# Sequence 0's chosen rows transposed by VectorE from gathered quarter rows, and a regular order of step 4's values

## The chip, the cores and the metric

The kernel runs on one core of a Trainium2 chip. The metric is the device time of one launch in microseconds; before the change its median over 3 runs is 431.92 us (431.19 to 432.13). All data are float32.

## The reference, cut to what matters

```python
# attention: 8 sequences, 12 heads, 448 tokens, head size 64
scores = q @ k.T / sqrt(64) - log(448)
x = sigmoid(scores) @ v                  # heads joined: x is (8, 448, 768)
# mixture of depths, for each sequence b
s = x[b] @ w_gate                        # one score for each token
top_idx = argpartition(-s, 128)[:128]    # the 128 best tokens
xe = x[b, top_idx]                       # (128, 768): the "chosen rows"
ye = relu(xe @ w1) @ w2                  # w1 (768, 1024), w2 (1024, 768)
out[b, top_idx] = xe + sigmoid(s[top_idx])[:, None] * ye
out[b, others] = x[b, others]
```

## The kernel before, in words

**Steps and slots.** Attention is done in 12 steps (s = 0 to 11), each on two groups of four heads. A step has 7 slots (n = 0 to 6). A slot makes scores on TensorE into two PSUM tiles of two banks each, `PA[0]` and `PA[1]` (`score`, L387, matmuls on L397), ScalarE turns each tile by a sigmoid into `attn` (`squash`, L402, L411), and TensorE multiplies earlier `attn` tiles with v into four PSUM banks `PO[x][pr]` (`value`, L416, L429). The values run behind the scores: the values of step s run from slot 4 of step s to slot 3 of step s+1. A score call uses half of the 128 rows of TensorE's array and a value call the other half, so that a score and a value can run side by side; two scores of the same `pr` or two values of the same half go one after the other.

**Three orders of values.** `slot` (L856) has: (1) the regular order of `rounds` (L777), in which one slot near the end of a step's values is split (`split`, L785): there both halves of the values are started before the scores and ended after them; (2) for the steps in `LATE` (L788), `first_slots` and `last_slot` with the tables `LOW` and `HIGH`; (3) one for step 0. `LATE` is steps 4 to 10 before the change. For steps whose successor is in `BLOCKS` (L706) the split is the last slot, otherwise the last but one. When all values of a step are in, VectorE transposes them out of `PO` into `x_b` (`take`, L447, L453). TensorE cannot write a bank of `PO` for the next step until that is done. `join` (L435) writes one element of each `PO` bank on ScalarE or VectorE, which fixes the order between engines.

**Blocks of the second part.** In slot 3 of steps 4 to 11, `block` (L736) runs takes, stores, parts of the gate and the items of `BLOCKS[s]`: ("t", b) transposes the chosen rows of sequence b, (1, p, key) and (2, p, key) are quarter-size products of the first and second matrix for a pair p of sequences (seven products in place of eight, by sums of quarters). Each item takes PSUM banks from `places`. Step 4 held only ("t", 0), and step 5 held (1, 0, 1) and (1, 0, 2), 48 matmuls together.

**Chosen rows.** `fetch(b)` (L540) on VectorE makes the list of 128 token numbers `idx`; `gather(b)` reads these rows of 3072 bytes from `out` into `xe`, by an indirect DMA issued on GpSimd. `turn_rows` (L568) transposes `xe` by six TensorE transposes of 128 columns each (L580) into two PSUM banks, which ScalarE copies into the tile `rows_t` (L582, L583); a third ScalarE instruction makes the gate (L585). In the transpose, `xe` is the stationary operand and the identity the moving one. `rows_t` also serves as v of steps 1 and 3, so it is free only when the values of step 3 are done.

**Order.** The whole order is written out by hand (`tc.manual_schedule`): each engine works through its own list in the order of the calls. DMAs go out on SP's queue (loads of q, k, weights; stores), on GpSimd's (ranks, gathers) and a few on ScalarE's. `after` (L973) says what follows each slot.

Of the kernel before, what the change touches and what calls it, by code (L numbers as in the profile page):

```python
# [17 lines left out]
def kernel(  # L18
# [170 lines left out]
    def load_v(s, pairs_too=None):  # L189


        if s >= NS:
            return
        if s == 0 and not pairs_too:
            t = raw_v[s]
        elif s in (1, 3):
            t = moe.tile([P, 6 * KH * P], F32, name="rows_t")[:, :4 * NU * Dh]
        elif s == min(BLOCKS) + 1:
# [33 lines left out]
    sums = {}  # L232
    lent = {}

    def quarter(m, i, j):

        if m == 1:
            return moe_w1[j * KH * P:(j + 1) * KH * P, i * FH * P:(i + 1) * FH * P].rearrange(
                "(t p) c -> p t c", p=P)
        return moe_w2[i * FH * P:(i + 1) * FH * P, j * DH:(j + 1) * DH].rearrange(  # L240
            "(t p) c -> p t c", p=P)

    HELD1, HELD2 = ((0, 0), (0, 1), (1, 1)), ((0, 0), (1, 0), (1, 1))

    def load_quarter(m, dst, at):
        nc.sync.dma_start(out=dst.rearrange("p (t c) -> p t c", t=KH if m == 1 else FH),
                          in_=quarter(m, *at))

    def load_held(m, x):
        load_quarter(m, (w1_sb, w2_sb)[m - 1][:, x], (HELD1, HELD2)[m - 1][x])  # L250
# [77 lines left out]
    who = [const.tile([P, NC], F32, name=f"who{x}") for x in range(2)]  # L328
    tokens = const.tile([P, TB, TT], F32, name="tokens")
    slot_s = const.tile([P, 1], F32, name="slot_s")  # L330
    gate_s = const.tile([P, TT], F32, name="gate_s")
    place_s = const.tile([P, TT], F32, name="place_s")

    def constants():
        make_identity(nc, iden)
        nc.gpsimd.iota(slot_s, pattern=[[0, 1]], base=0, channel_multiplier=1,
                       allow_small_or_imprecise_dtypes=True)

        for t in (gate_s, *who):
            nc.gpsimd.memset(t, 0.0)  # L340
        nc.gpsimd.memset(place_s, float(S))
        nc.gpsimd.iota(tokens, pattern=[[1, TB], [TB, TT]], base=0, channel_multiplier=0,
                       allow_small_or_imprecise_dtypes=True)
# [196 lines left out]
    def fetch(b):  # L540
# [4 lines left out]
        for x, t in enumerate((tokens.rearrange("p r t -> p (r t)"), st[b]["rep"])):  # L545
# [4 lines left out]
        nc.vector.tensor_scalar(out=idx[:n], in0=got[:n, 0:1], scalar1=float(b * S),  # L550
                                scalar2=None, op0=ALU.add)
        st[b].update(idx=idx, picked=got[:, 1:2])
        gather(b)

    def gather(b):
# [9 lines left out]

    pairs = {}

    def turn_rows(b, both):  # L568


        n = CAP
# [4 lines left out]
        x = pairs[p]["x"]  # L576
        ps = [t.rearrange("p (k n) -> p k n", n=P) for t in both]
        for t in range(KD):
            a, i = divmod(t, KH)
            nc.tensor.transpose(ps[a][:, i, :n], st[b]["xe"][:n, t * P:(t + 1) * P],  # L580
                                iden[:n, :n])
        nc.scalar.activation(x[:, 2 * odd, :, :n], ps[0][:, :KH, :n], AF.Copy)  # L582
        nc.scalar.activation(x[:, 2 * odd + 1, :, :n], ps[1][:, :KH, :n], AF.Copy)  # L583
        st[b]["gate"] = moe.tile([P, 1], F32, name="gate", bufs=4)
        nc.scalar.activation(st[b]["gate"][:n], st[b]["picked"][:n], AF.Sigmoid,  # L585
                             scale=1.0 / GATE_UP)
        if not odd:
            return
        for dst, y, z in ((4, 2, 0), (5, 3, 4), (2, 3, 2)):
# [108 lines left out]
    def scatter(b):  # L698
# [5 lines left out]


    BLOCKS = {  # L706
# [29 lines left out]
    def block(s):  # L736

        places = [PO[0][0], PO[0][1], PA[1][:, 0], PA[0][:, 0], PO[1][0], PO[1][1], PO[1][0]]
        if s == NF + 1:
            places = [PA[1][:, 0], PO[0][0]]  # L740
        elif s == NF + 2:
            places = [PO[0][0], PO[1][0]]
        for x in range(2):
            takes(s - 1, x)
        if (s, NF) in FETCHED and s > NF + 3:
# [31 lines left out]
    def rounds(s):  # L777


        same = [(0, 0, 1), (1, 0, 1), (1, 2, 3), (0, 2, 3), (0, 4, 5)]  # L780
        if s + 1 in BLOCKS:
            return same + [(1, 4, 5), (1, 0, 6)]
        return same + [(0, 1, 6), (1, 4, 5)]

    def split(s, i):  # L785
        return i == (6 if s + 1 in BLOCKS else 5)

    LATE = range(min(BLOCKS), NS - 1)  # L788
# [67 lines left out]
    def slot(s, n):  # L856
# [22 lines left out]
        if vs in LATE and n == NF:  # L879
            last_slot(s, n)  # L880
            return
        if vs and vs not in LATE and split(vs, i):
            one, two, u = rounds(vs)[i]
            for half in range(2):
                value(vs, half, one, u)
# [87 lines left out]
    def after(s, n):  # L973

        if n == NF and s:
# [5 lines left out]
            if s in BLOCKS:  # L981
                block(s)
            else:
                stores(s, n)
            if s == 2:
                gates(2 * s - 2, own=False)
            else:
                turn("q", 2 * s + 2)
# [45 lines left out]
            keep_sum(m, key)  # L1034
        if (s, n) in MADE:
            make_sum(*MADE[s, n])
        for b in range(B - 1):
            full = FULL[b]
            if (s, n) == ((4, 0) if b == 1 else (full, 5 + b % 2)):
                spread(b)  # L1040
            if (s, n) == RANKED[b]:
                ranking(b)
# [67 lines left out]
```

## Time and profile before

| What | us |
|---|---|
| median of 3 runs | 431.92 (431.19 to 432.13) |
| the profiled execution | 434.43 |
| its span, first to last instruction | 432.6 |
| TensorE matmul busy in the span | 424.7 (98%) |
| VectorE busy | 281.6 (65%) |
| ScalarE busy | 190.3 (44%) |
| GpSimd busy | 48.0 (11%) |
| granted TensorE clock, mean | 1.000 |

The profiled execution is some 2.5 us longer than the median of the timed runs; 1.8 us of it lie outside its span. A step of the attention part shows as 14 sigmoids of ScalarE; the distance from one sigmoid to the same one of the next step is the length of a step, and reads any change of a step directly. TensorE runs several small matmuls at once, so its busy share says little: lost time shows as a longer distance between such marks, not as idle time.

### The profile page before, as it was taken

To read this page: it belongs to the slowest core of one execution; us is meant where nothing else is said; L and a number is where in the kernel's file an instruction comes from. 1 tells how busy PE (TensorE), PEld (TensorE's weight loads), DVE (VectorE), ACT (ScalarE), POOL (GpSimd) and SP (SyncE) were. 2 spreads that over 40 slices of the span, in tenths; PEclk is the share of its full clock that TensorE was granted. 3 is DMA by queue.
4 is the path that set the end of the run, shared out by engine and by line. 5 is a ranking of instruction groups with operands and counts; after the bars stand their busy time and mean duration, and the time that the engine had idled before them with its cause. 6 is when DMAs were issued, how large, how long until landed. Compare 5 with 4: busy or idle time off the path is not lost.

```text
span 432.6 us, 14250 instructions
## 1 busy us (share of the span) xinstructions
PE 424.7 (98%) x6324; PEld 254.7 (59%) x6324; DVE 281.6 (65%) x597; ACT 190.3 (44%) x249; POOL 48.0 (11%) x81
## 2 busy tenths in 40 slices
PE   8999999999999999999999999999999999999995
PEld 3455453545666478465447549546545859769952
DVE  4427557583967776976968636755666648983472
ACT  4666656666664633650660651563264330101100
POOL 3000001210210020100302020010020110101001
PEclk9999999999999999999999999999999999999999
DMA  6896747899863997988566887399935981821001
GB/s 191 245 273 178 285 89 155 207 209 251 252 180 74 244 296 186 261 269 204 182 224 184 240 204 152 103 265 277 264 109 116 236 241 36 162 57 77 23 1 73
DMA packets 114937, 78.64 MB, mean 182 GB/s; under 512 B 91420, under 2 KB 100892, under 8 KB 114876
## 3 DMA queue, kind: packets, MB, share of 16 engines
q1 hardware_dynamic: 107948, 62.47, 55.0%
q0 software_dynamic: 3296, 9.54, 7.6%
q10 hardware_dynamic: 3632, 5.74, 5.4%
q8 instruction: 49, 0.80, 0.8%
q14 instruction: 12, 0.10, 0.1%
HBM read 57.25 MB, written 20.48 MB: 180 GB/s over the span
## 4 chain that ended last, share of the span: by engine, by line
PE 93%; DMA 3%; ACT 1%; issue 1%; SPq 1%; DVE 1%; POOLq 0%; ACTq 0%
PE a L397 30%; PE o L429 28%; PE o L616 11%; PE o L680 11%; PE a L616 6%; PE a L680 5%; DMA rows_t<-in_k_dram 1%; DMA raw_k<-in_k_dram 1%; PE o L580 1%; ACT attn L411 1%; DMA out_dram<-xe,idx 1%; SPq L219 0%; PE a L580 0%; POOLq L1105 0%; SPq L120 0%
## 5 line engine op out<-in xcount | busy, mean ns | idle before, releaser
L397 PE MATMUL a<-qT,kT 32*64 32x448 f32 x2624 | 244.9, 537 | 0.9 <-DVE kT L153 0.5
L411 ACT ACTIVATE attn<-a,bias_s 128x896 f32<-128x896 f32 x162 | 161.4, 1007 | 86.1 <-PE a L397 81.7
L429 PE MATMUL o<-attn,raw_v 32*64 32x448 f32 x1952 | 176.6, 537 | 0.1
L397 PEld LDWEIGHTS a<-qT,kT 32*64 32x64 f32 x2624 | 95.6, 131 | 90.3 <-ACT attn L411 52.8
L429 PEld LDWEIGHTS o<-attn,raw_v 32*64 32x64 f32 x1952 | 69.5, 131 | 29.3 <-issue 22.5
L453 DVE STREAM_TRANSPOSE x_b<-o 128x448 f32<-128x448 f32 x48 | 28.1, 626 | 53.6 <-PE o L429 37.3
L429 PE MATMUL o<-attn,rows_t 32*64 32x448 f32 x448 | 41.9, 538 | 0.0
L632 ACT ACTIVATE hidden<-hidden 128x512 f32<-128x512 f32 x12 | 7.5, 630 | 65.8 <-DVE hidden L629 65.8
L629 DVE TENSOR_TENSOR hidden<-o,hidden 128x512 f32<-128x512 f32 x23 | 15.2, 687 | 24.2 <-PE o L616 24.0
L464 DVE TENSOR_REDUCE gate_p<-scr 128x14 f32<-128x448 f32 x48 | 29.8, 621 | 1.7
L461 DVE TENSOR_TENSOR scr<-x_b,wg_b 128x448 f32<-128x448 f32 x48 | 29.5, 615 | 1.1
L385 DVE STREAM_TRANSPOSE kT<-raw_k 128x448 f32<-128x448 f32 x42 | 24.1, 611 | 4.0 <-PE a L397 3.7
L376 DVE STREAM_TRANSPOSE qT<-qT 128x896 f32<-128x896 f32 x22 | 23.8, 1083 | 4.2 <-DMA qT<-in_q_dram 3.5
L616 PE MATMUL o<-rows_t,spare 128*128 128x128 f32 x216 | 25.6, 276 | 0.0
L616 PEld LDWEIGHTS o<-rows_t,spare 128*128 128x128 f32 x216 | 24.8, 192 | 1.4 <-DVE x_b L453 1.4
L680 PE MATMUL o<-spare,hidden 128*128 128x384 f32 x72 | 24.3, 487 | 0.0
L691 DVE SCALAR_TENSOR_TENSOR xe<-o,gate,xe 128x384 f32<-128x384 f32 x29 | 16.6, 612 | 9.7 <-PE o L680 9.6
L519 DVE SCALAR_TENSOR_TENSOR scr<-rep,who,tie 128x448 f32<-128x448 f32 (+1 forms) x28 | 18.9, 677 | 4.9 <-DMA rep<-scores 4.2
L535 POOL DMA_DIRECT2D ranks<-turned x28 | 14.5, 525 | 67.0 <-DVE turned L532 67.0
L429 PEld LDWEIGHTS o<-attn,rows_t 32*64 32x64 f32 x448 | 17.0, 131 | 5.7 <-issue 5.2
L429 PE MATMUL o<-attn,hidden 32*64 32x448 f32 x224 | 20.2, 535 | 0.0
L616 PEld LDWEIGHTS o<-rows_t,w_sb 128*128 128x128 f32 x168 | 19.3, 192 | 1.0 <-DVE x_b L453 0.7
(118 smaller groups left out, 392.7 us busy)
## 6 DMA issues: line engine op xcount, KB each, us to landing
qT<-in_q_dram SPq DMA_DIRECT2D x24, 448.0 KB
out_dram<-x_b SPq DMA_DIRECT2D x32, 336.0 KB
raw_k<-in_k_dram SPq DMA_DIRECT2D x21, 448.0 KB
spare<-sum SPq DMA_DIRECT2D x18, 384.0 KB
sum<-spare SPq DMA_DIRECT2D x8, 768.0 KB
raw_v<-in_v_dram ACTq DMA_DIRECT2D x24, 224.0 KB
w_sb<-in_moe_w_dram SPq DMA_DIRECT2D x6, 768.0 KB
rows_t<-in_v_dram SPq DMA_DIRECT2D x8, 224.0 KB
```

Source lines behind the costliest of these rows:

```text
L376: nc.vector.transpose(heads["q", i], heads["q", i])
L385: nc.vector.transpose(kt[:, e], t[:, e].rearrange("p (a n) d -> p n a d", a=2))
L397: nc.tensor.matmul(out[y * Dh:(y + 1) * Dh, h % 2, :S], kt[d, e, r:r + 2].rearrange("d r t -> d (r t)"), qt[d, e], start=(e == 0), stop=(e ...
L411: nc.scalar.activation(a, psc[:, :, :S], AF.Sigmoid, bias=bias_s, scale=QK_SCALE)
L429: nc.tensor.matmul(PO[x][pr][j * Dh:(j + 1) * Dh, :S], raw_v[s][rows, 2 * pr + j, at:at + Dh], attn[s, pr, n][rows, j, :], start=((s, x, p ...
L453: nc.vector.transpose(x_tiles[b][:, :, 2 * g + pr, :], PO[x][pr][:, :S].rearrange("p (r t) -> p r t", t=TT))
L461: nc.vector.tensor_tensor(out=tmp, in0=x_tiles[b][:, :, hp, :], in1=wg_b[:, hp:hp + 1, :].to_broadcast([P, TB, TT]), op=ALU.mult)
L464: nc.vector.tensor_reduce(out=gate_parts[b][:, :, hp], in_=tmp, axis=AX.X, op=ALU.add)
L519: nc.vector.scalar_tensor_tensor(out=junk[:n], in0=rep[:n], scalar=own, in1=tie[:n], op0=ALU.subtract, op1=ALU.is_gt, accum_out=place_s[:n ...
L616: nc.tensor.matmul(ps[:, f, :n], w((t * FH + f) * P, P), x[:, t, :n], start=(t == 0), stop=(t == KH - 1))
L680: nc.tensor.matmul(ps[:n, :DH], h[:, t, :n], w(t * DH, DH), start=(t == 0), stop=(t == FH - 1))
L691: nc.vector.scalar_tensor_tensor(out=xe[:n, cols], in0=ps[:n, :DH], scalar=st[b]["gate"][:n, 0:1], in1=xe[:n, cols], op0=ALU.mult, op1=ALU ...
```

## The change

1. `rows_t` of sequence 0 is no longer made by TensorE. After slot 3 of step 4, `gather_parts(0)` issues four indirect DMAs on GpSimd. They gather quarter rows (192 floats, 768 bytes) of the 128 chosen tokens into the last third of `rows_t`, so that group g of 32 partitions holds quarter g. After slot 6 of step 4, `turn_parts(0)` lets VectorE transpose all 128 x 768 elements in 32 x 32 blocks into the first third of `rows_t`, reading with a step of 6 elements. The gather of whole rows into `xe` stays (it is needed for the sum at the end).
2. For the indices of the quarters, `fetch(0)` has eight more small VectorE instructions (seven copies, one multiply and add), and the setup four more GpSimd memsets.
3. This transposition puts element 6p + c of a row on partition p of block c, where the old one put element 128c + p. So the first matrix is loaded with its rows in the same order (`load_quarter`, still pieces of 2 KB), and `turn_rows` of the sequences 1 to 7 now reads its stationary operand with a step of 6 elements (24 bytes) in place of 1.
4. The block of step 4 is gone. `LATE` begins at step 5: step 4's values run in the regular order. Step 3's values are now split in the last slot but one, as those of steps 1 and 2, and step 4's in the last.
5. The block of step 5 takes its first two banks as `PA[1][:, 0]`, `PO[0][0]` (as step 4's block did) in place of `PO[0][0]`, `PO[1][0]`.

```diff
+        for g in range(4):
+            nc.gpsimd.memset(part_s[g * TT:(g + 1) * TT], float(g))
...
     def load_quarter(m, dst, at):
-        nc.sync.dma_start(out=dst.rearrange("p (t c) -> p t c", t=KH if m == 1 else FH),
-                          in_=quarter(m, *at))
+        if m == 2:
+            nc.sync.dma_start(out=dst.rearrange("p (t c) -> p t c", t=FH), in_=quarter(*at))
+            return
+        i, j = at
+        nc.sync.dma_start(
+            out=dst.rearrange("p (t c) -> p t c", t=KH),
+            in_=bass.AP(tensor=moe_w1.tensor, offset=moe_w1.offset + j * KH * F + i * FH * P,
+                        ap=[[KD * F, P], [F, KH], [1, FH * P]]))
...
+        if b == 0:
+            four = moe.tile([P, 4], F32, name="four")
+            for j in range(4):
+                nc.vector.tensor_copy(four[:TT, j:j + 1], got[j * TT:(j + 1) * TT, 0:1])
+            for g in range(1, 4):
+                nc.vector.tensor_copy(four[g * TT:(g + 1) * TT], four[:TT])
+            st[b]["idx4"] = idx4 = moe.tile([P, 4], I32, name="idx4")
+            nc.vector.tensor_scalar(out=idx4, in0=four, scalar1=4.0, scalar2=part_s,
+                                    op0=ALU.mult, op1=ALU.add)
...
+    def gather_parts(b):
+
+        w = open_pair(b)[2][:, 4:6].rearrange("p m k n -> p (m k n)")
+        for j in range(4):
+            nc.gpsimd.indirect_dma_start(
+                out=w[:, j * D // 4:(j + 1) * D // 4], out_offset=None,
+                in_=out[:b + 1].rearrange("b s (g c) -> (b s g) c", g=4),
+                in_offset=bass.IndirectOffsetOnAxis(ap=st[b]["idx4"][:, j:j + 1], axis=0))
+
+    def turn_parts(b):
+
+        x = pairs[b // 2]["x"]
+        nc.vector.transpose(
+            x[:, :2].rearrange("p m k (j t) -> p (m k) j t", j=4),
+            x[:, 4:6].rearrange("p m k n -> p (m k n)").rearrange(
+                "p (j d c) -> p c j d", j=4, c=KD))
+        row_gate(b)
...
-            nc.tensor.transpose(ps[a][:, i, :n], st[b]["xe"][:n, t * P:(t + 1) * P],
+            nc.tensor.transpose(ps[a][:, i, :n], st[b]["xe"][:n, t::KD],
                                 iden[:n, :n])
...
     BLOCKS = {
-        4: [("t", 0)],
         5: [(1, 0, 1), (1, 0, 2)],
...
-        if s == NF + 1:
+        if s == NF + 2:
             places = [PA[1][:, 0], PO[0][0]]
-        elif s == NF + 2:
-            places = [PO[0][0], PO[1][0]]
...
-        if s + 1 in BLOCKS:
-            return same + [(1, 4, 5), (1, 0, 6)]
-        return same + [(0, 1, 6), (1, 4, 5)]
+        return same + ([(1, 4, 5), (1, 0, 6)] if s == NF + 1 else [(0, 1, 6), (1, 4, 5)])
-
-    def split(s, i):
-        return i == (6 if s + 1 in BLOCKS else 5)
-
-    LATE = range(min(BLOCKS), NS - 1)
+    LATE = range(NF + 2, NS - 1)
...
-        if vs and vs not in LATE and split(vs, i):
+        if vs and vs not in LATE and i == 5 + (vs == NF + 1):
...
+            if s == NF + 1:
+                gather_parts(0)
...
+        if (s, n) == (NF + 1, NU - 1):
+            turn_parts(0)
```

More of the change, by code (lines that the diff above doesn't have):

```diff
@@ L197, in load_v @@
             t = moe.tile([P, 6 * KH * P], F32, name="rows_t")[:, :4 * NU * Dh]
-        elif s == min(BLOCKS) + 1:
+        elif s == NF + 2:
             t = hidden(0)[:, 3 * FH * P:3 * FH * P + 4 * NU * Dh]
@@ L233, with quarter @@
     lent = {}
[L235 to L239, printed above, removed]
+    def quarter(i, j):
         return moe_w2[i * FH * P:(i + 1) * FH * P, j * DH:(j + 1) * DH].rearrange(
@@ L330 @@
     slot_s = const.tile([P, 1], F32, name="slot_s")
+    part_s = const.tile([P, 1], F32, name="part_s")
     gate_s = const.tile([P, TT], F32, name="gate_s")
@@ L566, with open_pair @@
     pairs = {}
-    def turn_rows(b, both):
-        n = CAP
+    assert CAP == P and D == 4 * KD * TT
+    def open_pair(b):
         p, odd = divmod(b, 2)
@@ L575, in turn_rows, with row_gate @@
             pairs[p] = {"x": t.rearrange("p (m k n) -> p m k n", m=6, k=KH)}
-        x = pairs[p]["x"]
+        return p, odd, pairs[p]["x"]
+    def gather_parts(b):
[12 more added lines that the diff above has]
+        row_gate(b)
+    def row_gate(b):
+        n = CAP
+        st[b]["gate"] = moe.tile([P, 1], F32, name="gate", bufs=4)
+        nc.scalar.activation(st[b]["gate"][:n], st[b]["picked"][:n], AF.Sigmoid,
+                             scale=1.0 / GATE_UP)
+    def turn_rows(b, both):
+        n = CAP
+        p, odd, x = open_pair(b)
         ps = [t.rearrange("p (k n) -> p k n", n=P) for t in both]
@@ L583, in turn_rows @@
         nc.scalar.activation(x[:, 2 * odd + 1, :, :n], ps[1][:, :KH, :n], AF.Copy)
-        st[b]["gate"] = moe.tile([P, 1], F32, name="gate", bufs=4)
-        nc.scalar.activation(st[b]["gate"][:n], st[b]["picked"][:n], AF.Sigmoid,
-                             scale=1.0 / GATE_UP)
+        row_gate(b)
         if not odd:
```

## The prediction

> **What bounds the kernel.** I read the page first (busy shares, chain of waits), then ScalarE's timeline, which is a clock for the steps, then all engines around the two places that the change touches, last the groups by form for prices.
>
> ```profile
> PE 424.7 (98%) x6324; PEld 254.7 (59%) x6324; DVE 281.6 (65%) x597; ACT 190.3 (44%) x249; POOL 48.0 (11%) x81
> ...
> PE 93%; DMA 3%; ACT 1%; issue 1%; SPq 1%; DVE 1%; POOLq 0%; ACTq 0%
> ```
>
> TensorE ends the chain nearly throughout. A gain must shorten TensorE's own list or a wait in it; what other engines save counts only there. The next lines are the first sigmoid of slot 6 in steps 2, 3, 4 and 5:
>
> ```profile
> 67.74 1.01 ACT L411 ACTIVATE attn<-a,bias_s 128x896 f32<-128x896 f32 x1 [0.54 <-PE a L397]
> ...
> 89.79 1.01 ACT L411 ACTIVATE attn<-a,bias_s 128x896 f32<-128x896 f32 x1 [0.54 <-PE a L397]
> ...
> 113.90 1.01 ACT L411 ACTIVATE attn<-a,bias_s 128x896 f32<-128x896 f32 x1 [0.56 <-PE a L397]
> ...
> 140.72 1.01 ACT L411 ACTIVATE attn<-a,bias_s 128x896 f32<-128x896 f32 x1 [0.52 <-PE a L397]
> ```
>
> From 2 to 3 are 22.05 us, from 3 to 4 24.11, from 4 to 5 26.82, the last with 48 matmuls of the block in it. (From 1 to 2, from a mark at 45.31: 22.43.) A slot in steady work takes 3.01 us (64.72 to 67.74), a step of seven without loss 21.06. So a regular boundary costs 1.0 (2 to 3), the one with the transposes 3.05. The boundary of 4 to 5 costs 26.82 - 5.56 - 21.06 = 0.2, if the block is taken as the 5.56 us below.
>
> TensorE, ScalarE and VectorE at the two places:
>
> ```profile
> 103.96 0.55 PE L580 MATMUL a<-iden,xe 128*128 128x128 f32 x3
> 104.12 2.25 DVE L453 STREAM_TRANSPOSE x_b<-o 128x448 f32<-128x448 f32 x4 [7.62 <-ACT attn L411]
> ...
> 104.82 0.55 PE L580 MATMUL o<-iden,xe 128*128 128x128 f32 x3 [0.32 <-DVE x_b L453]
> ...
> 105.30 0.98 PE L397 MATMUL a<-qT,kT 32*64 32x448 f32 x8
> 105.41 0.49 ACT L583 ACTIVATE rows_t<-o 128x384 f32<-128x384 f32 x1 [0.37 <-PE o L580]
> ...
> 105.95 0.70 PE L429 MATMUL o<-attn,raw_v 32*64 32x448 f32 x4
> ```
>
> ```profile
> 127.25 5.62 PE L616 MATMUL o<-rows_t,w_sb 128*128 128x128 f32 x48
> 132.81 0.60 PE L397 MATMUL a<-qT,kT 32*64 32x448 f32 x4
> 132.83 0.61 PE L429 MATMUL o<-attn,hidden 32*64 32x448 f32 x4
> ```
>
> At step 4 the transposes take 1.34 us from their first start to the next score, with a wait for VectorE's take inside. Values start 0.65 later, because ScalarE's copy L583 must empty `PO[0][0]`. At step 5, scores and values start together.
>
> [...]L616's loads last 192 ns each, yet 24 of its matmuls take 2.68 us in the chain, 112 ns each.[...]
>
> ```profile
> L616 PEld LDWEIGHTS o<-rows_t,w_sb 128*128 128x128 f32 x168 | 19.3, 192 | 1.0 <-DVE x_b L453 0.7
> ...
> L580 PEld LDWEIGHTS o<-iden,xe 128*128 128x128 f32 x30 | 3.4, 141 | 2.3 <-DVE x_b L453 2.0 <-issue 0.2
> ```
>
> ```profile
> L464 DVE TENSOR_REDUCE gate_p<-scr 128x14 f32<-128x448 f32 x48 | 29.8, 621 | 1.7
> ...
> L487 DVE TENSOR_REDUCE total<-parts 32x32 f32<-32x128 f32 x8 | 2.9, 362 | 0.3
> ...
> L480 DVE TENSOR_REDUCE gate_s<-gate_p 128x14 f32<-128x84 f32 x8 | 1.9, 236 | 0.2
> ```
>
> L464 and L480 read neighbours: (621 - 236) / (448 - 84) = 1.06 ns an element. L487 reads 128 elements 128 bytes apart; on that line it would take 283 ns and takes 362. So it pays 1.68 ns an element, 1.6 times as much.
>
> **Step 4.** The block goes and the boundary becomes a regular one. Its price is that of 2 to 3, or at worst of 1 to 2: 22.05 to 22.43. I take 22.05, because VectorE is idle ahead of the takes (7.62 us above). Gain 24.11 - 22.05 = 2.06.
>
> **Step 5.** Its boundary becomes what step 4's was, a split last slot followed by a block and `first_slots`, with other contents in the block. From 24.11 I take out the 1.34 and put in the 5.56: 28.33. Then the bank: `PO[0][0]` now holds the second product, which is emptied by VectorE's add L629, not by a ScalarE copy. That add starts at 132.99, 0.18 after the next score, lasts 0.69, and the hand-over takes 0.05 as at 105.90 to 105.95. So values start 0.92 after the first score, 0.27 later than the 0.65: 28.60. VectorE is in time for the add: its takes end 2.5 us after the values do, four gate operations (L461, L464) add 2.6, and the block lasts 5.6. The takes themselves lie beside the first product, since that starts in `PA[1]`. Loss 28.60 - 26.82 = 1.78.
>
> Sum of both: -2.06 + 1.78 = -0.28; with 22.43, +0.10. I take -0.2.
>
> **What lies beside.** The eight small VectorE operations in `fetch(0)`: seven at 0.16 to 0.17 (L501, L485) and one at 0.15 (L550), 1.3 us in the idle 7.62. They delay the next transposition of k and thereby SP's next load of k (issued at 96.53) by 1.3, and SP's stores and v loads queued behind it; that k is needed only at 107.28, and v of step 5 at 132.8. Four GpSimd gathers at 1.06 each (as L562 at 95.71) are 4.2 us. GpSimd is idle 15.41 us there, and the rank DMAs behind them start at 113.46. A gather lands after 6.7 us, so with `rows_t` free 22.05 after step 2's last values (which give way to `rows_t` at 81.7), the last is in at about 103.7 + 4.2 + 6.7 = 114.6. VectorE comes to the transposition near 117 (118.2 now, with takes that end 1.2 earlier in the regular order). It costs 0.93 (L376's 1083 ns for 896 elements, scaled to 768) to 1.4 (at 1.68 ns an element). VectorE waits 3.10 us for ranks at 124.10 in the profile, and this covers it; without that cover the takes of step 5 would slip by as much, with 2.7 us of the first product before TensorE needs a bank and 0.5 before the add. ScalarE loses two copies and keeps the gate. The load of the first matrix has as many pieces of the same size: nothing.
>
> **The strided weight loads** are the unknown: 42 transposes (7 sequences of 6). They start 0.109 apart today (six in 0.66 at 341.27 in the chain)[...]. A load of 64 columns (L397) lasts 131 ns, one of 128 (L616) 192, so 70 are fixed, and L580's 141 hold 71 ns of reading, under the 109. If the 1.6 applies as a ratio, 113 ns: +0.004 each, 0.2 in all. Doubled, 142: 0.033 each, 1.4 in all. If a line costs TensorE the same 1.68 ns as VectorE, 215: 0.106 each, 4.4 in all. From below nothing[...]. I take nothing[...] and keep 4.4 for the range.
>
> Forecast: -0.2 on the profiled execution's 434.43, so 434.2; on the median of the runs, which is 2.5 lower, 431.7. That is within 0.2% (0.86 us), about what a measurement here can tell from no change.
>
> **Rivals.** *A: slower, by the strided loads.* Place: L580 in sequences 1 to 7. From 0.109 us of reading on, each further ns counts 42 times; beyond 134 ns it passes +0.86. For it: the reduction at 1.68 ns[...]. At 142 ns 433.1, at 215 ns 436.1; I take 435. *B: faster, step 5 keeps its cheap boundary.* The split's waits would lie under the block's 5.6 us. The 2.06 would stay whole: 429.9; or half of the loss: 430.8. Against: at step 4 the split's lost beats lie before the block and the delayed values behind it, neither under it. *C: the gather is late.* VectorE would then come late to ranks, takes and the add; each us beyond the 0.5 delays step 5's values, so takes 1.3 us late give 432.5. Against: 2.4 us until VectorE comes, and its 3.10 us wait after it. *D: it doesn't do what it says*: the transposes of sequence 0 still cost; excluded, since TensorE's list has 42 of them left of 48.
>
> **Numbers.** Forecast 0.40, A 0.34, B 0.22, C 0.04. The forecast's own range is 431.2 to 432.7. For 8 in 10 I go down to 430.5 (half of B) and up to 436.0 (nearly all of A). Faster: B and a little of the forecast, 0.25. Slower: A, half of C and a little of the forecast, 0.38. The same: 0.37.
>
> **What would show it.** The slot-6 marks: 3 to 4 about 22.1 and 4 to 5 about 28.6 us. L580's weight loads: up to 180 ns recorded means hidden, 250 and more means A, with transposes more than 0.11 apart. The first value of step 5 (L429) 0.9 us after the first score behind the block. VectorE's wait ahead of the new transposition: none. I am wrong if the second mark interval stays below 28, if the transposes spread, or if a new wait for `rows_t` stands before L616.

## The result, and the profile after

The changed kernel takes 434.50 us (median of 7 runs, 432.99 to 436.45), the kernel before 432.13 us beside it (7 runs, 431.08 to 432.73). The ratio is 1.0064 with a 95% interval of 1.0041 to 1.0086: slower by 1.8 to 3.7 us. The forecast was no change (431.7 us).

The profiled execution of the changed kernel is its fastest (432.99 us), that of the kernel before is well above its median (434.43). Side by side the two profiles say the opposite of the medians, so I compare stages and not spans: from step 5 to step 10 alone the profile before took 176.44 us and that of the changed kernel 174.04, a difference for which the change gives no reason. From the page of the changed kernel, busy time and the chain of waits:

```profile
PE 423.0 (98%) x6318; PEld 250.4 (58%) x6318; DVE 284.1 (66%) x606; ACT 189.4 (44%) x247; POOL 52.5 (12%) x89
...
PE 88%; DMA 5%; DVE 2%; ACT 2%; issue 1%; POOL 1%; POOLq 0%; SPq 0%; DVEq 0%; ACTq 0%
```

TensorE has the 6 matmuls less that the change takes away. But its share of the chain fell from 93% to 88%, and DMA's rose from 3% to 5%: somewhere TensorE now waits for a transfer. The marks, the first sigmoid of slot 6 in steps 2 to 5 (ScalarE's timeline):

```profile
67.13 1.01 ACT L417 ACTIVATE attn<-a,bias_s 128x896 f32<-128x896 f32 x1 [0.54 <-PE a L403]
...
89.17 1.01 ACT L417 ACTIVATE attn<-a,bias_s 128x896 f32<-128x896 f32 x1 [0.54 <-PE a L403]
...
111.21 1.01 ACT L417 ACTIVATE attn<-a,bias_s 128x896 f32<-128x896 f32 x1 [0.49 <-PE a L403]
...
141.04 1.01 ACT L417 ACTIVATE attn<-a,bias_s 128x896 f32<-128x896 f32 x1 [0.56 <-PE a L403]
```

| interval of slot 6 (us) | before | forecast | after |
|---|---|---|---|
| step 2 to 3 | 22.05 | 22.05 | 22.04 |
| step 3 to 4 (block taken away) | 24.11 | 22.05 | 22.04 |
| step 4 to 5 (split before the block) | 26.82 | 28.60 | 29.83 |

Step 4 gave 2.07 us, as forecast. Step 5 lost 3.01 and not 1.78. Where the missing 1.23 us come from is seen in the timeline behind block 5 (columns: start, length, engine and line, tile, and in brackets the idle time before it and what ended that):

```profile
126.39 0.69 DVE L553 SCALAR_TENSOR_TENSOR scr<-hot,slot_s,tokens 128x448 f32<-128x448 f32 x1 [4.55 <-DMA hot<-ranks]
...
127.80 2.23 DVE L459 STREAM_TRANSPOSE x_b<-o 128x448 f32<-128x448 f32 x4
...
131.50 0.98 PE L403 MATMUL a<-qT,kT 32*64 32x448 f32 x8
...
132.42 0.68 DVE L673 TENSOR_TENSOR hidden<-o,hidden 128x512 f32<-128x512 f32 x1
...
133.16 0.61 PE L435 MATMUL o<-attn,hidden 32*64 32x448 f32 x4 [0.68 <-DVE hidden L673]
```

The first value (L435) comes 1.66 us after the first score (L403), not 0.92. It waits for VectorE's add L673. The add has no idle time before it: VectorE was simply late, because its takes (L459) began at 127.80 behind the picking of sequence 1's rows (L553, in `fetch(1)`), which waited 4.55 us for the ranks. Before, that wait was 3.10 and ended at 124.10. The chain of the changed kernel names the two transfers (start, length, what):

```profile
113.22 6.40 DMA ranks<-turned
...
120.15 6.14 DMA hot<-ranks
```

The ranks went out 1.8 us earlier than before (issue at 111.65, not 113.46) and landed later: the hop into `hot` was issued at 120.15, before at 118.61. They now go out 0.49 us behind a load of 768 KB of weights (issued at 111.16), before 4.64 behind it (108.82), with loads of q and k beside. That these loads hold them up is likely, but not shown.

The late picking is not the whole of it. Where the picking is in time (e9, e13 and others below) step 5 takes 28.39 us, 1.44 less than here. Of these, 0.74 are the value that comes 1.66 and not 0.92 after the score. The other 0.70 lie ahead of block 5 (14.73 us from step 4's mark to the block, 14.03 in e9, e13 and e18): TensorE stands still ahead of 119.53, with no wait shown. With the picking in time it would still lose these 0.70 us. Its weight loads there:

```profile
119.53 0.14 PEld L435 LDWEIGHTS o<-attn,raw_v 32*64 32x64 f32 x4 [0.96 <-issue]
```

The strided weight loads, one line of the changed kernel (forms of the transposes with their durations, minimum, median and maximum in ns):

```profile
L626 PEld LDWEIGHTS o<-iden,xe x27: 209/237/243, 154.5 to 384.9; 128*128 128x128 f32 x27
L626 PE MATMUL o<-iden,xe x27: 273/300/401, 154.6 to 385.1; 128*128 128x128 f32 x27
```

A load is recorded with 237 ns in place of 141. In the chain, six transposes took 0.66 us before and take this now:

```profile
339.19 0.81 PE o L626 x6
```

0.135 us each in place of 0.110, that is, some 0.025 more for each of 42: 1.1 us.

### The profile page after: what moved, and what is told of

Read it like the earlier page. It is cut to its first block, busy times and chain, and to the rows that moved or that the text cites. A ratio compares the mean times of both kernels' runs of the same rounds, so it can differ in the third digit from the quotient of the medians.

```text
span 431.2 us, 14274 instructions
## 1 busy us (share of the span) xinstructions
PE 423.0 (98%) x6318; PEld 250.4 (58%) x6318; DVE 284.1 (66%) x606; ACT 189.4 (44%) x247; POOL 52.5 (12%) x89
## 4 chain that ended last, share of the span: by engine, by line
PE 88%; DMA 5%; DVE 2%; ACT 2%; issue 1%; POOL 1%; POOLq 0%; SPq 0%; DVEq 0%; ACTq 0%
PE a L403 27%; PE o L435 27%; PE o L724 11%; PE o L660 10%; PE a L660 6%; PE a L724 5%; DMA ranks<-turned 1%; DMA hot<-ranks 1%; PE o L626 1%; DMA rows_t<-out_dram,idx 1%; ACT hidden L417 1%; DMA qT<-in_q_dram 1%; DMA out_dram<-xe,idx 1%; POOL rows_t L597 1%; ACT attn L417 1%
## 5 line engine op out<-in xcount | busy, mean ns | idle before, releaser
L403 PE MATMUL a<-qT,kT 32*64 32x448 f32 x2624 | 243.5, 538 | 0.1
L435 PE MATMUL o<-attn,raw_v 32*64 32x448 f32 x1952 | 175.2, 537 | 0.4 <-issue 0.4
L403 PEld LDWEIGHTS a<-qT,kT 32*64 32x64 f32 x2624 | 93.0, 131 | 90.5 <-ACT attn L417 54.2
L435 PEld LDWEIGHTS o<-attn,raw_v 32*64 32x64 f32 x1952 | 66.5, 131 | 31.5 <-issue 28.0
L459 DVE STREAM_TRANSPOSE x_b<-o 128x448 f32<-128x448 f32 x48 | 27.9, 625 | 43.3 <-PE o L435 31.6
L435 PE MATMUL o<-attn,rows_t 32*64 32x448 f32 x448 | 41.8, 538 | 0.0
L470 DVE TENSOR_REDUCE gate_p<-scr 128x14 f32<-128x448 f32 x48 | 29.8, 622 | 1.7
L673 DVE TENSOR_TENSOR hidden<-o,hidden 128x512 f32<-128x512 f32 x23 | 15.2, 687 | 22.4 <-PE o L660 22.2
L435 PE MATMUL o<-attn,hidden 32*64 32x448 f32 x224 | 20.4, 535 | 0.7 <-DVE hidden L673 0.7
L435 PEld LDWEIGHTS o<-attn,rows_t 32*64 32x64 f32 x448 | 16.6, 131 | 6.6 <-issue 6.3
L724 PEld LDWEIGHTS o<-spare,hidden 128*128 128x128 f32 x72 | 13.6, 190 | 10.0 <-DVE x_b L459 0.7
```

Of the source, the lines that this page charges most:

```text
L403: nc.tensor.matmul(out[y * Dh:(y + 1) * Dh, h % 2, :S], kt[d, e, r:r + 2].rearrange("d r t -> d (r t)"), qt[d, e], start=(e == 0), stop=(e ...
L435: nc.tensor.matmul(PO[x][pr][j * Dh:(j + 1) * Dh, :S], raw_v[s][rows, 2 * pr + j, at:at + Dh], attn[s, pr, n][rows, j, :], start=((s, x, p ...
L459: nc.vector.transpose(x_tiles[b][:, :, 2 * g + pr, :], PO[x][pr][:, :S].rearrange("p (r t) -> p r t", t=TT))
L470: nc.vector.tensor_reduce(out=gate_parts[b][:, :, hp], in_=tmp, axis=AX.X, op=ALU.add)
L724: nc.tensor.matmul(ps[:n, :DH], h[:, t, :n], w(t * DH, DH), start=(t == 0), stop=(t == FH - 1))
```

## The experiments

Theory at the start: the order of the work (parts 4 and 5) nets to nothing, as forecast; the loss is strides (S), the late ranks (T, as above), or the four gathers (G), each of which I had costed at nothing. All ratios are against the kernel before on the same chip in the same stretch of time. The last two columns are intervals from the profile of that run, 24.11 and 26.82 in the kernel before. e1 to e4, e17 and e18 ran on one and the same chip.

| run | what | ratio (95%) | 3 to 4 | 4 to 5 |
|---|---|---|---|---|
| e1 | before + strides | 1.0032 (1.0017 to 1.0048) | 24.24 | 26.82 |
| e2 | after, no strides | 1.0106 (1.0075 to 1.0137) | 27.86 | 28.39 |
| e3 | after, no gathers | 1.0013 (0.9994 to 1.0031) | 22.60 | 28.44 |
| e4 | order only | 0.9997 (0.9978 to 1.0016) | 22.86 | 29.89 |
| e17 | after, one gather for four | 1.0031 (1.0016 to 1.0047) | 22.31 | 29.80 |
| e18 | after | 1.0088 (1.0067 to 1.0109) | 30.24 | 28.39 |
| e5 | after | 1.0037 (1.0018 to 1.0056) | 22.05 | 29.86 |
| e6 | before + gathers | 1.0053 (1.0028 to 1.0078) | 24.46 | 27.61 |
| e7 | after, gathers later | 1.0056 (1.0038 to 1.0075) | 22.54 | 31.89 |
| e8 | e7, no strides | 1.0040 (1.0022 to 1.0059) | 22.54 | 29.93 |
| e9 | after, picking in slot 4 | 1.0110 (1.0089 to 1.0131) | 23.14 | 28.38 |
| e10 | e9, no strides | 1.0092 (1.0070 to 1.0115) | 22.10 | 28.81 |
| e11 | before, picking in slot 4 | 1.0066 (1.0042 to 1.0090) | 24.74 | 26.95 |
| e12 | e6, picking in slot 4 | 1.0088 (1.0070 to 1.0106) | 24.04 | 28.36 |
| e13 | after, picking behind block 5 | 1.0156 (1.0114 to 1.0199) | 25.35 | 28.39 |
| e14 | e2 again | 1.0106 (1.0061 to 1.0151) | 25.36 | 29.89 |
| e15 | e13, no strides | 1.0132 (1.0092 to 1.0172) | 25.56 | 30.47 |
| e16 | e6, picking behind block 5 | 1.0152 (1.0107 to 1.0198) | 27.33 | 27.57 |

### Taking the change apart

**e1: the strides alone.** The kernel before with the first matrix loaded in the new order and the stationary operand read with a step of 24 bytes, in all 48 transposes.

```diff
-            nc.tensor.transpose(ps[a][:, i, :n], st[b]["xe"][:n, t * P:(t + 1) * P],
+            nc.tensor.transpose(ps[a][:, i, :n], st[b]["xe"][:n, t::KD],
```

> The kernel before with point 3 of the change alone: the first matrix in the new row order, and all 48 transposes of TensorE reading their stationary operand 24 bytes apart. Theory S (strided weight loads slow TensorE): in the changed kernel's profile the transposes stand 0.135 us apart instead of 0.109, so 48 x 0.026 = 1.25 us, ratio to before about 1.003; recorded weight loads 237 ns instead of 141. Theory R (the loss of the changed kernel comes from the rank DMAs of step 4, which land late because of the quarter gathers and the shifted loads): no gathers here, so ratio 1.000 and the spread of the runs as before. Theory B (the new boundary of steps 4 to 5 costs more in itself): ratio 1.000.

Measured 1.0032: 1.4 us (0.7 to 2.1). From the profile, 48 x 0.025 = 1.2. The strides are not hidden: e1's weight loads are recorded with 229 to 235 ns on the mean, in place of 140 to 141.

**e2: the changed kernel without strides.**

```diff
-            nc.tensor.transpose(ps[a][:, i, :n], st[b]["xe"][:n, t::KD],
+            nc.tensor.transpose(ps[a][:, i, :n], st[b]["xe"][:n, t * P:(t + 1) * P],
```

> The changed kernel with the old reads in the transposes (neighbouring elements), all else kept. Left out: the order of the elements of the chosen rows of sequences 1 to 7 no longer fits the order of the first matrix's rows, so their results differ from the reference. Theory S: 42 x 0.026 = 1.1 us come back: from 434.5 to about 433.4, ratio to before 1.003. If S were the whole loss: 432.1, ratio 1.000. Theories R and B: almost nothing comes back, ratio 1.005 to 1.006.

A miss, and the most useful one: with a cost taken away the kernel came out at 1.0106. The marks place it: 27.86 us from step 3 to 4, where the changed kernel has 22.04 and where no transpose is left. This pointed to the gathers. The transposes themselves did become cheaper: their weight loads are recorded with 141 ns again, and six take 0.66 us.

**e3 and e4: no gathers; order alone.** In e3 GpSimd fills the quarter rows with a constant in place of the four gathers; e4 also drops the index operations and the strides, so that points 4 and 5 of the change are left.

```diff
-        for j in range(4):
-            nc.gpsimd.indirect_dma_start(
...
+        nc.gpsimd.memset(w, 0.5)
```

> The changed kernel with the four quarter gathers replaced by one GpSimd memset of the same tile; the index operations and VectorE's transposition stay. Left out: the chosen rows of sequence 0 do not reach the products. Theory R: the rank DMAs of sequence 1 are no longer slowed, the list of ranks (hot) lands before VectorE asks for the takes of step 5, and the first value of step 5 starts 0.9 us after the first score behind the block instead of 1.66: at least 0.7 us back, in the slower runs more, so 433.5 or less, ratio 1.003 or less, and a smaller spread. Theory S: nothing back, 434.5. Theory B: nothing back; values still start 1.66 after the score.

> Points 4 and 5 of the change alone: new order of step 4's values and step 5's block in a bank of scores, reads of neighbours, no gathers (a memset instead), no index operations; VectorE's transposition stays. Left out: the chosen rows of sequence 0 do not reach the products, and the row order of the others does not fit the first matrix. Theories S and R together: what is left is the sum of the prediction, -0.28 us: about 431.9, ratio 0.999, with slot-6 marks 22.05 and 28.6 us apart. Theory B: the second interval stays near 29.8 us, and the kernel stays above before by 0.9 us, ratio 1.002.

e4 is at 0.9997, where the forecast's sum of -0.28 us is 0.9994. e3 is at 1.0013. On this chip, then, the order costs nothing that can be told from zero (-1.0 to +0.7 us), and the strides 0.7 (e3 less e4, with intervals of 0.8 us to either side of each) to 1.4 us (e1). From step 3 to 4 both profiles are 0.5 to 0.8 us over 22.05. In e4 TensorE halts there, without any gather of the change (columns as before; "issue" is time without a wait that the profile knows):

```profile
94.77 0.14 PEld L435 LDWEIGHTS o<-attn,rows_t 32*64 32x64 f32 x3 [0.60 <-issue]
```

### The gathers

**e5 and e6.** The changed kernel again, and the kernel before with nothing but the index operations and the gathers, which land in slots that nobody reads.

```diff
             if s in BLOCKS:
                 block(s)
             else:
                 stores(s, n)
+            if s == NF + 1:
+                gather_parts(0)
```

> The changed kernel itself, nothing edited: a yardstick on the same chip as the other three. Measured earlier on another occasion: ratio 1.0064. Theory A+G (strided reads about +0.3%, gathers about +0.4%, order of work about 0): 1.005 to 1.008 again. If it comes near 1.010, the no-stride layout's 1.0106 was the chip or the occasion and not the layout; if it comes under 1.004, the first measurement carried something that isn't the kernel's.

> The kernel before plus the eight small VectorE instructions for the quarter indices and the four gathers at the same place as in the change; they land in free slots that nobody reads, and all transposes stay as before. Theory G (the gathers and their quarter rows, [...]beside the loads that already fill the transfer engines, hold up what TensorE needs next): +1.3 to +4 us, ratio 1.003 to 1.009, with TensorE standing without a shown wait in 104 to 117 us. Theory R (the loss of the changed kernel is strided reads and the later ranks alone): 1.000 +- 0.0015. My forecast costed this at nothing.

e6 is slower by 2.3 us (1.2 to 3.4) with nothing of the change but gathers and their indices: G is confirmed in the total, and R (the gathers cost nothing) is out. Not confirmed is the place: its profile, one of its faster executions (433.30 us), has no halt of TensorE between 104 and 117 us beyond the wait at its block; what it shows is a halt of 0.69 us ("issue") at 129.24, inside block 5. e5, with all of the change, is at 1.0037, no slower than e6: with intervals as wide as these the costs can't be added up from single runs.

**e7 and e8: the same gathers later.** Issued behind the four small rank transfers, for which GpSimd waits 6.4 us in the changed kernel anyway; VectorE's transposition moved to slot 2 of step 5. e8 also drops the strides.

```diff
+        if b == 1:
+            gather_parts(0)
         st[b]["ranks"] = every = moe.tile([P, NC * P], F32, name="hot")[:, :S]
...
-        if (s, n) == (NF + 1, NU - 1):
+        if (s, n) == (NF + 2, 2):
             turn_parts(0)
```

> The changed kernel with the four gathers moved behind the four small transfers of the ranks of sequence 1 (about 8 us later, in a stretch where GpSimd waits 6 us for those transfers anyway), and VectorE's transposition moved from the end of step 4's last slot to step 5's slot 2. Theory G: the gathers no longer meet the three loads of 98 to 111 us, so the ratio falls to that of the kernel without gathers, 1.001 to 1.003. Rival (the gathers cost the same wherever they stand): as the changed kernel again, 1.005 to 1.008. Either way step 4's boundary stays at 22.1 us.

> The kernel with the late gathers, and the chosen rows of the other sequences read by TensorE as neighbouring elements again (the weights stay in the new order, so the results of sequences 1 to 7 no longer fit the reference). Theory A+G: without the strides' 1.1 to 1.4 us and without the gathers' collision what is left is the order of the work, 0.998 to 1.000. Rival (leaving the strides out makes the kernel slower by itself, as 1.0106 against 1.0064 seemed to say): over 1.004.

No gain: 1.0056 and 1.0040. The profile of e7 shows why the test was a bad one (VectorE's timeline, then the takes it holds up):

```profile
126.57 1.53 DVE L607 STREAM_TRANSPOSE rows_t<-rows_t 128x768 f32<-128x768 f32 x1 [6.29 <-DMA rows_t<-out_dram,idx]
...
129.40 2.23 DVE L459 STREAM_TRANSPOSE x_b<-o 128x448 f32<-128x448 f32 x4
```

I had put a wait of 6.29 us for the gathers in front of the takes; step 5 became 31.89 us. It is rival C of the forecast, made by hand, and with it the runs tell nothing of where the gathers cost.

**e17 and e18: one gather or four.** On one chip the changed kernel, and the changed kernel with one gather of 128 whole rows in place of four of 128 quarter rows: the same bytes at the same place.

```diff
-        for j in range(4):
-            nc.gpsimd.indirect_dma_start(
-                out=w[:, j * D // 4:(j + 1) * D // 4], out_offset=None,
...
+        nc.gpsimd.indirect_dma_start(
+            out=w, out_offset=None, in_=rows_to(b),
+            in_offset=bass.IndirectOffsetOnAxis(ap=st[b]["idx"][:, 0:1], axis=0))
```

> The changed kernel with one gather of 128 whole rows (3 KB each) in place of the four of 128 quarter rows (768 bytes each): same bytes, place and queue, a quarter of the instructions and pieces (the chosen rows of sequence 0 then lie in another order than VectorE's transposition wants, so sequence 0's results don't fit). Theory P (pieces and GpSimd instructions do the harm): ratio near that of the kernel without gathers, 1.001 to 1.003, and at least 0.003 under e18. Theory B (bytes and place do it): within 0.002 of e18.

> The changed kernel again, nothing edited, beside e17 on one chip. From the two measurements: 1.0037 to 1.0064. If the size of the gathers' cost goes with the occasion, as the 1.0106 of the kernel without strides says, up to 1.013; a profile with the loss then shows under 50 matmuls in a stretch of 3 us between 104 and 113 us.

1.0031 against 1.0088, with intervals apart: on this chip the four small gathers cost 2.5 us more than one large one. (The profiled execution of e18 is its slowest, 441.19 us for a median of 439.12; that of e17, 434.13, is one of its faster ones.) Where it goes is seen when the stretch is cut into pieces of 3 us (columns: stretch, its length, PE's busy time and number of matmuls, granted clock, DMA share, GB/s). The changed kernel in its first profile:

```profile
104.00:107.00 3.00, 3.00 (x72) 1.00 0.62 123
107.00:110.00 3.00, 3.00 (x72) 1.00 1.06 162
110.00:113.00 3.00, 3.00 (x72) 1.00 0.99 230
113.00:116.00 3.00, 3.00 (x72) 1.00 1.06 252
```

The same kernel as e18:

```profile
104.00:107.00 3.00, 3.00 (x59) 1.00 1.07 159
107.00:110.00 3.00, 2.17 (x11) 1.00 0.94 186
110.00:113.00 3.00, 2.54 (x21) 0.51 1.09 213
113.00:116.00 3.00, 3.00 (x41) 0.50 1.03 235
```

And e17:

```profile
104.00:107.00 3.00, 3.00 (x68) 1.00 1.15 233
107.00:110.00 3.00, 3.00 (x72) 1.00 0.85 132
110.00:113.00 3.00, 3.00 (x72) 1.00 1.01 228
113.00:116.00 3.00, 3.00 (x72) 1.00 1.05 276
```

Undisturbed, as in the first profile, TensorE executes 72 matmuls in 3 us. In e18 it executes 11 and 21 in the two stretches while and after GpSimd gathers, and the busy column hardly shows it (2.17 of 3 us), since the ends of matmuls are modelled. Then the granted clock falls to one half, from 110.07 to 116.90 us, and from 113 to 116 us TensorE executes 41. Step 3 to 4 takes 30.24 us here, 8.20 more than 22.04. By 110 us TensorE is 74 matmuls behind (13 and 61), 3.1 us at 24 in a microsecond; by 116 us 82 more (51 and 31), 3.4 us, in which the end of the stall and the half clock overlap. Some 0.9 us were lost earlier, in a halt at 94 us, ahead of the first gather (104.55). Not every stall brings the half clock: e13 to e16, with 25 to 52 matmuls in the stretches from 107 to 113 us, keep a clock of 1.00. The column of the DMA share doesn't tell the three apart: 0.94 to 1.09 in e18, and up to 1.06 and 1.15 in the two without a stall. GpSimd's gathers of e18, and two of the weight loads that came dribbling:

```profile
107.12 0.95 POOL L597 DMA_INDIRECT rows_t<-out_dram,idx  x1 [0.30 <-issue]
108.37 0.95 POOL L597 DMA_INDIRECT rows_t<-out_dram,idx  x1 [0.30 <-issue]
```

```profile
109.03 0.16 PEld L403 LDWEIGHTS a<-qT,kT 32*64 32x64 f32 x2 [1.24 <-issue]
109.76 0.13 PEld L403 LDWEIGHTS a<-qT,kT 32*64 32x64 f32 x1 [0.57 <-issue]
```

"issue" means that the profile knows of no wait: no semaphore, no operand. TensorE goes through its list one or two instructions at a time. e2, e13, e14, e15 and e16 show the same, with 25 to 38 matmuls in their worst stretch between 107 and 113 us; the first profile of the changed kernel, e5, e6, e9, e10 and e12, which also have the four gathers here, don't. The six with the stall are all the profiles with these gathers from two chips (e2 and e18 from one, e13 to e16 from the other); e5, e6, e9, e10 and e12 come from two other chips. All six executions of e18 took 437.3 us or more, all twenty of e5 437.0 or less. So it goes with the chip or with the occasion; which of them isn't shown. No profile without the four gathers at this place (before, e1, e3, e4, e7, e8, e11, e17) has it in this size.

### The late ranks

**e9 to e12: the picking in slot 4.** One entry of a table puts `fetch(1)` behind the takes of step 5, in four kernels: the changed one, without strides, the kernel before, and e6.

```diff
-    FETCHED = {(3, 6): 0, (5, 2): 1, (6, 3): 2, (8, 3): 3, (9, 5): 4, (11, 2): 5}
+    FETCHED = {(3, 6): 0, (5, 4): 1, (6, 3): 2, (8, 3): 3, (9, 5): 4, (11, 2): 5}
```

> The changed kernel with one entry of a table altered: the picking of sequence 1's rows, which waits for the ranks, is done in slot 4 of step 5 and not in slot 2, so VectorE's takes, which step 5's block waits for, no longer stand behind a wait for a transfer. Theory T (the 1.2 us by which step 5's boundary came out longer than forecast is VectorE reaching the takes late, because the ranks' transfer lands late): the interval from step 4's to step 5's slot 6 falls from 29.8 to 28.4-28.6 us, total about 1.3 us under the changed kernel, ratio 1.001 to 1.003. Rival G (the gathers delay TensorE itself): interval stays at 29.3 or more, ratio 1.004 to 1.006.

> As the run before it, and TensorE reads the chosen rows of sequences 1 to 7 as neighbouring elements again (the weights stay in the new order, so their results no longer fit the reference). Theory: what is left is the order of work alone, -2.07 + 1.6 us, and the strides' 1.1 to 1.4 us are gone too: ratio 0.998 to 1.000, interval of step 5 28.4 to 28.6 us, the six-slot steps with turned rows about 0.15 us per turning shorter. If theory T is wrong: 1.001 to 1.004.

> Control: the kernel before with the same one entry of the table altered. There the takes wait for TensorE's values and not for the picking (0.30 us for TensorE at 125.89), so nothing should change: ratio 0.9985 to 1.0015, interval of step 5 26.8 us. If this too becomes faster by 0.3%, the late picking is a cost of both kernels and explains nothing of their difference.

> The kernel before plus quarter indices and gathers (as in the run that measured 1.0053), with the picking of sequence 1 moved to slot 4 of step 5. Theory T (the gathers cost by holding up the ranks, and these by holding up the takes): 0.999 to 1.002, interval of step 5 back at 26.8 from 27.6 us. Rival G: 1.004 to 1.006 as without the move.

In its place the theory holds: VectorE's takes in e9 wait for TensorE and no longer for ranks, the first value comes 0.92 us after the first score, and step 5 is 28.38 us, where it was 29.8 with the picking ahead of the takes (0.70 of the difference is the halt of TensorE, which e9 doesn't have; e10, with a part of it, has 28.81). The control e11 stays at 26.95. In the total all four are slower, the control too (1.0066). e9's timelines of GpSimd and VectorE:

```profile
144.71 2.28 POOL L577 DMA_INDIRECT xe<-out_dram,idx  x1 [4.55 <-DVE idx L556]
146.97 0.61 POOL L517 DMA_DIRECT2D rep<-scores  x1
```

```profile
153.89 0.69 DVE L525 SCALAR_TENSOR_TENSOR scr<-rep,who,tie 128x448 f32<-128x448 f32 x1 [4.91 <-DMA rep<-scores]
```

The gather of sequence 1's rows now stands on GpSimd ahead of the copies of scores (`rep`), VectorE waits 4.91 us for these in front of the takes of step 6 (2.47 in the kernel before), and the next interval grows to 38.00 us (39.00 in e11, 35.93 before). What was won in step 5 was lost in step 6. e12's step 5 did not come back to 26.8 but stayed at 28.36, which T does not explain: TensorE halts twice in it with "issue", 0.77 us ahead of 122.00 and 0.59 ahead of 129.84.

**e13 to e16: the picking just behind block 5, and e2 again.**

```diff
             if s == NF + 1:
                 gather_parts(0)
+            if s == NF + 2:
+                fetch(FETCHED[s, NF])
```

> The changed kernel with the picking of sequence 1's rows placed in step 5 just behind block 5's adds, ahead of the transpositions of q and k (slot 4 was too late: GpSimd's gather then stood in front of the copies of scores and step 6 lost 2 to 4 us). Theory T: interval of step 5 28.4 to 28.7 us, the next one 35.3 to 35.9, ratio 1.0005 to 1.003. Rival: the scores of step 6 come 1.6 us later through VectorE, and step 6's interval takes back what step 5's gains: 36.5 to 37.3 us, ratio 1.004 to 1.006.

> The changed kernel with neighbouring reads by TensorE (the weights stay in the new order, so the results of sequences 1 to 7 don't fit the reference), a second time. If 1.0106 was that occasion's: 1.002 to 1.005 (the changed kernel's ratio less 0.003 for the strides). If it is the kernel's own: 1.008 to 1.013, with an interval of 27 to 28 us from step 3's to step 4's slot 6 again.

> Both edits together: picking behind block 5's adds, neighbouring reads (results of sequences 1 to 7 don't fit the reference). Theory: the order of work alone is left, -2.07 + 1.6 us: ratio 0.998 to 1.000. If gathers cost besides: 1.001 to 1.003.

> The kernel before plus quarter indices and gathers into free slots, with the picking of sequence 1 behind block 5's adds. Theory T: interval of step 5 26.8 to 27.1 us and total 0.999 to 1.002. If the gathers cost through TensorE's own starvation: 1.004 to 1.006, with the loss in 95 to 119 us (interval from step 3's to step 4's slot 6 24.5 us or more).

e14 repeated e2's 1.0106, on another chip. On that chip all four profiles lost 3.2 to 3.5 us between step 3 and 4 (25.35 to 25.56 for 22.05; e16 27.33 for 24.11), so the totals say nothing on the picking. e13's step 5 was again 28.39; its next interval 36.55, 0.74 above the changed kernel's 35.81, in the range that the rival had given for it. Three of four expectations missed, all for the gathers that I had taken to be settled.

## Why the prediction was wrong, point by point

- **What bounds the kernel: right.** TensorE's list and the waits in it decided everything; VectorE's and GpSimd's busy time did not.
- **Step 4, -2.06: right.** 22.04 in the first profile; 22.05 in e5.
- **Step 5, +1.78: right in its mechanism, and too small by 1.23 us in the first profile.** Where the picking is not in the way (e3, e9, e13) the interval is 28.38 to 28.44, close to the forecast's 28.60, and the value comes 0.92 us after the score, as forecast; where it is late (first profile, e4, e17) 29.80 to 29.89, and the value comes 1.66 to 1.72 us after it. (e5 and e14 have 29.86 and 29.89 for another reason: their takes wait for TensorE, which itself halts in this interval, for 1.33 us at 115.20 and 1.76 us at 118.70.) The step that failed is "The takes themselves lie beside the first product" together with the cover of 3.10 us at 124.10. I took that wait as slack for VectorE. It is a transfer that ends when it ends, and the kernel itself sends the ranks off earlier, into the loads of SP. e4 and e17 have it without the four gathers, so these are not its cause. The halt of 0.70 us ahead of the block, in the same three profiles, stood in no term of the forecast. I named the case in rival C, with its price (432.5 for takes 1.3 us late), but with another trigger, and gave it 0.04.
- **Order in total: right by the timing, 0.9997.** By the marks it should be -2.07 + 1.6 = -0.5 us with the picking in time and -2.07 + 3.0 = +0.9 us with it late. e4's interval (-1.0 to +0.7 us) holds the first and just misses the second; how often an execution has the one or the other stays open.
- **The strided loads: "I take nothing" was wrong.** Measured 0.025 us each and 1.1 us in all (e1: 1.4, 0.7 to 2.1), inside my bounds and next to the case "Doubled, 142" (1.4 us). The argument that failed is the "71 ns of reading, under the 109", an estimate of mine: with the new reads the transposes follow each other at 0.135 us, with the old ones in e2 again at 0.110. My split of a record into 70 ns fixed and the rest reading doesn't hold either, for it would make 167 ns of reading out of 237, and the transposes follow each other at 135. This is rival A's place; its price of 3.3 us, between the cases of 142 ns and of 215 (VectorE's 1.68 ns for each of 128 elements), was too high.
- **The gathers in a time in which "GpSimd is idle 15.41 us", taken as free: wrong, and the largest miss.** They landed before the 114.6 us of the forecast in the first profile, and VectorE had no wait for them. But GpSimd's idle time is not the whole price: TensorE, which waits for nothing of the gathers, falls behind beside them in e18. The price is 2.3 us in e6 and 2.5 us between e17 and e18. No rival had it. The chain before could show nothing of it: the kernel before has only gathers of whole rows, and in e17 one of these at the same place leaves TensorE at 68 to 72 matmuls a stretch.
- **VectorE's transposition**, forecast at 0.93 to 1.4 us, takes 1.60; it was not late in the first profile.

So the loss is made in two ways. In an execution without a stall, as the first profile, it is -2.07 + 3.01 + 1.1 = 2.0 us by the marks; the medians of that comparison are 2.4 apart. (This execution itself, at 432.99 us, is only 0.9 over the median before, so other parts of the kernel differ between executions by as much.) On the chip of e1 to e4, e17 and e18 it is 3.8 us, of which 0.6 are order and strides (e3) and 3.3 the gathers (e18 less e3).

**Still open:** through what the gathers stop TensorE. The pages of the kernel before and of the changed one list a queue of the kind "instruction" (q8) with 49 packets, 0.80 MB. Whether these are what is late isn't shown: in the trace of e14 two follow each other at 104.73 and 116.32 us, while TensorE dribbles from 106.8 to 110.8 and is back at its pace at 111: none lies at either end of the stall. The shorter halts with "issue" speak for them. Counted from the start of the kernel, they come after the same number of weight loads in different runs: 1750 (e2, e4, e9, e18), 2131 (e5, e14, e15, e16), 2259 (the first profile, e4, e10, e12, e17) and 2387 (e6, e12). That holds although e6, e12 and e16 still have the six transposes of sequence 0 in front, so it is the count and not the work that they have in common. The counts are 381, 128 and 128 apart, and 49 packets for 6318 loads make, as an estimate, one in 129 loads, if all are TensorE's. Such halts, of 0.58 to 2.34 us, come with and without the four gathers. The long stall of e2, e13 to e16 and e18 lies between about the 1970th and the 2000th load in each; its end fits the same count (2131 less 128 is 2003), its start doesn't. Why four gathers bring it on and one doesn't stays open. It wasn't tried to move a transfer of SP out of that stretch, which would tell whether the full transfer engines (a DMA share of 0.94 to 1.09 in e18) are needed for it. No run points to a version faster than both: the only ones not clearly slower than the kernel before are e3 and e4, which have no rows of sequence 0 to work on.

## What to carry to other kernels

Price a transfer by the stretch it falls into, and not only by the idle time of the engine that issues it: on the chip of e17 and e18, four small gathers cost 2.5 us more than one large one of the same bytes at the same place. A wait ahead of an engine is cover only while what it waits for stays put (here a wait of 3.10 us became one of 4.55); if the change moves the issue of that transfer, follow it to its landing. An operation that lies beside another is not free for that: next to weight loads recorded with 192 ns (L616) matmuls follow each other at 0.112 us, but with loads of 237 ns in place of 141 the transposes went from 0.110 to 0.135. Bound its price before writing nothing.

## What the runs showed of the hardware

- TensorE's weight load of 128 columns read 24 bytes apart is recorded with 237 ns in the changed kernel (L626) in place of 141 before (L580), and transposes follow each other at 0.135 us in place of 0.110.
- VectorE's transposition of 128 x 768 elements in blocks of 32 x 32, read 24 bytes apart, takes 1.53 us (e7) to 1.60 (changed kernel); 128 x 896 neighbours take 1.08 (both kernels).
- TensorE can lose 3 to 8 us from one step to the next (e13 to e16 3.2 to 3.5, e2 5.8, e18 8.2 with its half clock) with no wait shown, and a busy share of 98% beside it. The number of matmuls in a stretch (11 for 72) shows it at once.
- A stall of that kind is followed by a half clock (0.50) for 6.8 us in e18 and for 3.4 us in e2, and by none in e13 to e16.
- Shorter halts of TensorE without a shown wait, of 0.58 to 2.34 us, come after the same counts of its weight loads (1750, 2131, 2259, 2387) in different kernels.
